# Two gradient stores moved to a scatter by row numbers: a decode-step backward pass on one core

## The chip, the cores and the metric

The kernel runs on one core of one Trainium2 chip. The metric is device time in microseconds (us) of one execution. A core has a matrix engine (TensorE, PE in the profile), three elementwise engines (VectorE = DVE, ScalarE = ACT, GpSimd = POOL), a queue engine that here only issues transfers (SyncE = SP), and 16 DMA engines that move data between the chip's large memory and the on-chip memory of 128 partitions.

## The reference, cut to what matters

The program computes the output and the gradients of a gated mix of two branches for one token: `out = g * attention + (1 - g) * mlp`, with `g = sigmoid(sum(x * gate_w))`, all tensors in bfloat16.

```python
q = (x @ wq).reshape(B, 1, H, Dh)                    # x: 640, H = 32 heads, Dh = 128
p = softmax(q . k_cache * Dh ** -0.5)                # 4096 cached positions per head
a = (p . v_cache).reshape(B, 1, H * Dh) @ wo
act = h * tanh(log1p(exp(-|h|)) + max(h, 0));  h = x @ w1 + b1       # F = 1728
b = act @ w2
```

Returned are the output and the gradients of x, k_cache, v_cache, wq, wo, w1, b1, w2 and gate_w. The gradients of the caches are the bulk: 32 heads of 1 MiB each for K (output 2) and for V (output 3), as much as is read. dw2, the gradient of w2, is output 8, 1728 rows of 640: row i is the i-th activation times one row of 640 numbers that is the same for all.

## The kernel before, in words

One loop goes over the heads. For each head SyncE loads K and V (each 128 partitions x 8,192 B: partition p holds 32 positions), TensorE transposes them, forms score rows (line 538), ScalarE takes exponentials (line 575), VectorE makes the probabilities and their gradients (lines 587 to 593), TensorE multiplies them with K and V (line 631), and VectorE writes the outer products dK and dV (`outer`, line 598), each in two halves. `out_half` calls `outer` and, after the second half, issues the store on SyncE (line 616). There are four buffers for loaded K, four for loaded V, and four for results (`o_sb`). The last heads' results take freed K and V buffers instead, since nothing is loaded into them any more: dV of heads 29 to 31, dK of heads 28 to 30.

The order of the work is written out by hand; a scheduler adds the semaphore waits, and each engine runs its instructions in the written order. The MLP's steps are dealt out over the heads by a small list with costs (`mlp_some`); when its backward part is done, `dw2_some` computes dw2, two of its 14 column groups per head, on ScalarE (`m_dw2`, line 503). It writes dw2 over w2 in the tile `w2_sb`: partition p holds rows 13p to 13p + 12 in the groups 0 to 12 (16,640 B, one piece in the output too), and the last 64 rows stand in group 13. In the loop's pass for head 28 (`h == H - 4`) SyncE stores the first 1,664 rows in three transfers of 4, 4 and 5 groups (line 799), after that head's dV; GpSimd stores the last 64 rows (line 800) and db1 (line 802). GpSimd's own queue reaches line 800 as soon as group 13 is computed, far earlier.

In the same pass the gradients of wo and wq of the group of four heads before are made: four copies on ScalarE (`f_dwo`, line 380) just after that point, products on VectorE (lines 362 and 372). After the loop come head 31, the last group's wq and wo, and the final sums, whose three rows GpSimd stores (lines 920 to 922, 5 rows of 256 B each).

Constants (identity matrices, masks) are made by GpSimd and VectorE in the first 6 us, while the first loads run.

Of the kernel before, what the change touches and what calls it, by code (L numbers as in the profile page):

```python
# [8 lines left out]
ALU = mybir.AluOpType  # L9
AX = mybir.AxisListType  # L10
# [6 lines left out]
def kernel(  # L17
# [24 lines left out]
    nc = tc.nc  # L42
    P = 128
    _, H, Sk, Dh = A_k_cache.shape
# [8 lines left out]
    FR = F // P  # L53
    FM = FR * P
# [4 lines left out]
    W2P = [(0, 4), (4, 8), (8, FR)]  # L59
# [17 lines left out]
    dw2_v = out_8[0:FM, :].rearrange("(p fc) n -> p fc n", p=P)  # L77
# [11 lines left out]
    const = ctx.enter_context(tc.tile_pool(name="const", bufs=1))  # L89
# [59 lines left out]
    w2_sb = const.tile([P, FCN, D], BF16, name="w2_sb")  # L149
    for a, b in W2P:  # L150
# [7 lines left out]
    ident_bf = const.tile([P, P], BF16, name="ident_bf")  # L158
    nc.gpsimd.memset(ident_bf[:], 0.0)
    nc.gpsimd.affine_select(  # L160
        out=ident_bf[:], in_=ident_bf[:], compare_op=ALU.not_equal, fill=1.0,
        base=0, pattern=[[-1, P]], channel_multiplier=1,
# [20 lines left out]
    nc.vector.memset(aT_acc[:], 0.0)  # L183
    bT = const.tile([P, RC], F32, name="bT")
    dx_parts = const.tile([P, RC, NG + 3], F32, name="dx_parts")

    p4b, ds4b = [], []
    qz = const.tile([P, G, 2, 2, 16], BF16, name="qz")
# [57 lines left out]
    def g_qpair_cp(g):  # L246
        pair_cp(qz, groups[g].pop("pair"), 4)

    def g_docol(g):
        groups[g]["col"] = col_mm(groups[g]["do_row"])  # L250
# [163 lines left out]
    def m_np(fc):  # L414
        return P if fc < FR else FT
# [60 lines left out]
    def m_diag():  # L476
        nc.vector.tensor_copy(dh_bf[:, 0:FR], dh32[:, 0:FR])
        nc.vector.tensor_copy(dh_bf[0:FT, FR:FCN], dh32[0:FT, FR:FCN])
        nc.gpsimd.tensor_tensor(diag3, ident_bf[:].unsqueeze(2).to_broadcast([P, P, FR]),
                                dh_bf[:, 0:FR].unsqueeze(1).to_broadcast([P, P, FR]), ALU.mult)  # L480
        nc.gpsimd.tensor_tensor(mjunk[0:FT, FM:F], ident_bf[0:FT, 0:FT],
                                dh_bf[0:FT, FR:FCN].to_broadcast([FT, FT]), ALU.mult)
# [18 lines left out]
    def m_dw2(fc):  # L501
        n = m_np(fc)
        nc.scalar.activation(w2_sb[0:n, fc, :], db_bc[0:n, :], ACT.Copy, scale=act_f[0:n, fc:fc + 1])
# [14 lines left out]
    def ev():  # L518
        trq.pop(0)()
# [6 lines left out]
    def k_pe(h, c):  # L526
        if h < H:
            tr_pe(h, kts, KT, c)

    def v_pe(h, c):  # L530
        if h < H:
            tr_pe(h, vts, VT, c)
# [32 lines left out]
    def softmax(h):  # L565
        mx = s_ps.tile([P, P + 2], F32, name="mx", tag="mx")
        nc.tensor.transpose(mx[:, 0:P], dgms.pop(h)[:].to_broadcast([P, P]), ident_f[:])  # L567
        negM = small.tile([P, 1], F32, name="negM", tag="negM")
        nc.vector.tensor_reduce(negM[:], mx[:, 0:P], axis=AX.X, op=ALU.max, negate=True)  # L569
        return mx, negM  # L570

    def exps(h, negM):
        es[h] = small.tile([P, J], BF16, name="e_bf", tag="e_bf")
        zds[h] = small.tile([P, 2], F32, name="zd", tag="zd")
        nc.scalar.activation(es[h][:], sd[h][0], ACT.Exp, bias=negM[:], scale=scale, accum_out=zds[h][:, 0:1])  # L575
# [21 lines left out]
    def outer(dst, col4, row, a, b):  # L597
        nc.vector.tensor_tensor(  # L598
            dst[:, a:b, :].rearrange("p j (k t) -> p j k t", t=4),
            row.rearrange("p (k t) -> p k t", t=4).unsqueeze(1).to_broadcast([P, b - a, Dh // 4, 4]),  # L600
            col4[:, a:b, :].unsqueeze(2).to_broadcast([P, b - a, Dh // 4, 4]), ALU.mult)

    o_t = {}

    def out_half(w, h, dst, col4, row, k):
        hh = h % G
        if k == 0:
            if w == "k" and H - KBUFS <= h < H - 1:
                o_t[w, h] = kv_in.tile([P, J, Dh], BF16, name="Kn", tag="Kn")
            elif w == "v" and h > H - VBUFS:  # L610
                o_t[w, h] = kv_in.tile([P, J, Dh], BF16, name="Vn", tag="Vn", bufs=VBUFS)
            else:
                o_t[w, h] = outs.tile([P, J, Dh], BF16, name="o_sb", tag="o_sb")
        outer(o_t[w, h], col4, row[:, hh * Dh:(hh + 1) * Dh], k * JH, (k + 1) * JH)
        if k == 1:
            nc.sync.dma_start(dst[h], o_t.pop((w, h))[:])

    def dv_out(h, k):
        out_half("v", h, dVv, p4s[h], groups[h // G]["do_row"], k)
# [1 line left out]
    def dk_out(h, k):  # L621
        if h >= 0:
            out_half("k", h, dKv, ds4s[h], groups[h // G]["qs_row"], k)
# [12 lines left out]
    def dqo_red(h, x):  # L636
        if h >= 0:
            v = x[:].rearrange("p t r -> p (t r)")[:, 3:3 + 4 * (P - 1)].rearrange("p (s q) -> p s q", q=P - 1)
            nc.vector.tensor_reduce(groups[h // G]["dqo"][:, :, h % G],  # L639
                                    v[:, :, 0:P - 1:32].rearrange("p s (i c) -> p i s c", i=2),  # L640
                                    axis=AX.XY, op=ALU.add)
# [6 lines left out]
    m_cost = dict(h=0.8, b1=0.8, act=0.9, b=0.5, dh=0.9, diag=0.5, bc=0.5, dx=0.9, dw1=0.5, gap=0.0)  # L648
    m_fn = dict(h=m_h, b1=lambda i: (m_b1(), m_abs()), act=m_act, b=m_b, dh=m_dh,
                diag=lambda i: m_diag(), bc=m_bc, dx=m_dx, dw1=m_dw1)  # L650
    dw2_next = [0]

    def mlp_some(budget, pause=True):
        spent = 0.0
# [88 lines left out]
    for h in range(H - 1):  # L743
        g, hh = h // G, h % G
        nx, pv = g + 1 < NG, g > 0
        k_pe(h + 1, 2)
        ev()
        mx, negM = softmax(h)
        if hh == 3 and nx:
            g_qpair_cp(g + 1)  # L750
            g_docol(g + 1)
        dqo_red(h - 1, xs[h])
        k_pe(h + 1, 3)
        ev()
        exps(h, negM)
        dk_out(h - 1, 1)
        v_pe(h + 1, 0)
        if hh == 2 and nx:
            g_q(g + 1)
        v_pe(h + 1, 1)  # L760
        if hh == 3 and nx:
            g_dopair(g + 1)
            g_dopair_cp(g + 1)
        k_rows(h + 1)
        ev()
        ev()
        pjs(h)
        v_pe(h + 1, 2)
        ev()
        zd_mm(h, mx)  # L770
        if hh == 0 and pv:
            f_new(g - 1)
            f_diag(g - 1)
        elif h >= 2:
            mlp_some(0.9, False)
        v_pe(h + 1, 3)
        ev()
        probs(h, mx)
        if hh == 0 and pv:
            f_o4(g - 1)  # L780
            f_o4c(g - 1)
            f_bc(g - 1)
        dv_out(h, 0)
        k_pe(h + 2, 0)
        dq_o(h)
        v_rows(h + 1)
        rw_cp(h + 1)
        if h + 2 < H:
            ev()
        dv_out(h, 1)  # L790
        load_k(h + KBUFS)
        load_v(h + VBUFS)
        k_pe(h + 2, 1)
        if h + 2 < H:
            ev()
        if h == H - 4:
            assert dw2_next[0] == FCN
            for a, b in W2P:
                nc.sync.dma_start(dw2_v[:, a:b, :], w2_sb[:, a:b, :])
            nc.gpsimd.dma_start(out_8[FM:F, :], w2_sb[0:FT, FR, :])  # L800
            assert not any(k == "bc" for k, _ in mq)
            nc.gpsimd.dma_start(db1_row, dh_bc[0:1, :])
        if h == H - 2:
            assert not mq
            nc.sync.dma_start(dw1_v[:, 0:3, :], w1_sb[:, 0:3, :])
            nc.sync.dma_start(dw1_v[:, 3:RC, :], w1_sb[:, 3:RC, :])
        dk_out(h, 0)
        x_tr(h + 1)
        maxes(h + 1)
        if hh == 0:  # L810
            if nx:
                g_new(g + 1)
            if pv:
                l_pe(g - 1, 0, G)
                l_add(g - 1, g - 1, True)
                for t in range(G):
                    f_dwo(g - 1, t)
                f_dwo_st(g - 1)
                for c in range(2):
                    f_dx(g - 1, c)  # L820
                    f_dwq(g - 1, c)
        if hh == 1:
            if pv:
                for c in range(2, RC):
                    f_dx(g - 1, c)
                    f_dwq(g - 1, c)
                f_dwq_st(g - 1)
            if nx:
                w_pe("o", g + 1, 0)
                ev()  # L830
                w_pe("o", g + 1, 1)
                ev()
        if hh == 2:
            if g + 2 < NG:
                load_wo(g + 2)
            if not nx:
                for k in range(NWT):
                    w_pe("q", g, k)
                    ev()
            else:  # L840
                w_pe("o", g + 1, 2)
                ev()
                g_do(g + 1)
                g_qcol(g + 1)
                g_qpair(g + 1)
        if hh == 3:
            if g % 2 == 0 and g + 4 <= NG:
                load_wqp(g // 2 + 1)
            if nx:
                g_qs(g + 1)  # L850
        if h >= 2:
            mlp_some(0.9 if hh < 2 else 1.8)
            dw2_some(2)

    g, h = NG - 1, H - 1
# [97 lines left out]
```

## Time and profile before

| | us |
|---|---|
| median of 3 runs (404.71 to 405.26) | 404.71 |
| the profiled execution | 404.96 |
| its span, first to last instruction | 403.2 |
| DMA, busy share of q1 (SyncE's queue) over 16 engines | 98.1% |
| TensorE, VectorE, ScalarE busy | 305.9, 287.9, 232.4 |
| GpSimd busy | 11.8 |
| read and written in large memory | 82.03 MB each, 407 GB/s over the span |

The profile is one execution. Its page shows each engine's busy time, the span in 40 slices with a digit for the busy tenths, the DMA queues, the chain of work that ended last, and the costliest groups of instructions; lines such as L616 are lines of the kernel. Other views of the same trace give a timeline of one engine (start, length, engine, line, operation, out<-in, count, and in brackets the idle time before and what ended it), and tables of windows, one row for each stretch: its length, then busy time and count of PE, PEld (weight loads), DVE, ACT and POOL, TensorE's granted clock, the mean busy share of the 16 DMA engines, and GB/s. The trace also records each semaphore increment; a transfer signals its landing with 16 of them, one for each DMA engine, and the packets of each DMA queue with start, length and size.

### The profile page before, as it was taken

What the parts mean: (1) busy time and instruction counts of PE and PEld (TensorE: products, weight loads), DVE (VectorE), ACT (ScalarE), POOL (GpSimd) and SP (SyncE); (2) the same over time, 40 slices, a digit from 0 to 9 for tenths busy, and PEclk for the clock granted to TensorE, in tenths of its full rate; (3) what the DMA queues carried; (4) which work ended last, traced back from release to release, by engine and by line L of the source; (5) the groups of instructions that cost most, each with busy time, mean ns of one, the idle gap of its engine ahead of it and who ended that gap; (6) DMA issues with size and microseconds to landing.
All of it is one profiled execution on the core that took longest, in us unless ns stands there. A gap on an engine that the chain in (4) does not pass through costs nothing.

```text
span 403.2 us, 7688 instructions
## 1 busy us (share of the span) xinstructions
PE 305.9 (76%) x2930; PEld 207.0 (51%) x2945; DVE 287.9 (71%) x808; ACT 232.4 (58%) x468; POOL 11.8 (3%) x29
## 2 busy tenths in 40 slices
PE   2979989787897985876887779876886977677640
PEld 1556646464565663544555447544555645464420
DVE  2217738868678875769897956896997985679780
ACT  2466757754676563753668667765767655375220
POOL 3000001000000000000001200000000000000001
PEclk9999999988999998989998997988999899889555
DMA  7999999999999999999999999999999999999894
GB/s 274 428 416 423 417 424 415 417 423 424 422 422 426 423 414 424 424 418 428 422 423 428 424 418 424 427 418 423 422 419 424 425 417 425 426 422 377 360 389 153
DMA packets 28708, 164.55 MB, mean 408 GB/s; under 512 B 2991, under 2 KB 3056, under 8 KB 12288
## 3 DMA queue, kind: packets, MB, share of 16 engines
q1 hardware_dynamic: 28256, 163.97, 98.1%
q8 instruction: 23, 0.38, 0.4%
q0 software_dynamic: 384, 0.10, 0.1%
q14 instruction: 13, 0.11, 0.1%
q10 hardware_dynamic: 32, 0.01, 0.0%
HBM read 82.03 MB, written 82.03 MB: 407 GB/s over the span
## 4 chain that ended last, share of the span: by engine, by line
DMA 42%; PE 25%; DVE 22%; ACT 6%; issue 2%; POOL 0%; POOLq 0%; SPq 0%; DVEq 0%; ACTq 0%
DMA out_dram<-o_sb 40%; PE tr L515 9%; DVE o_sb L598 9%; PE rw L538 3%; PE rw L631 3%; DVE junk L362 3%; DMA wq_p<-in_A_wq_dram 2%; PE x L555 2%; DVE wq_p L372 2%; ACT rw_sb L549 2%; ACT do_row L266 2%; PE tr L324 2%; PE do_ps L263 1%; PE h_ps L405 1%; DVE mjunk L494 1%
## 5 line engine op out<-in xcount | busy, mean ns | idle before, releaser
L524 ACT COPY T<-tr 128x512 f32<-128x512 f32 x256 | 138.0, 595 | 53.0 <-PE tr L515 38.3
L598 DVE TENSOR_TENSOR o_sb<-qs_row,ds 128x2048 bf16<-128x2048 bf16 x58 | 70.8, 1220 | 37.6 <-DMA out_dram<-o_sb 37.5
L515 PE MATMUL tr<-ident_f,Kn 128*128 128x128 f32 x512 | 85.6, 295 | 5.8 <-DVE rw L508 5.8
L515 PE MATMUL tr<-ident_f,Vn 128*128 128x128 f32 x512 | 84.5, 299 | 6.6 <-ACT T L524 6.0
L515 PEld LDWEIGHTS tr<-ident_f,Vn 128*128 128x128 f32 x512 | 63.4, 154 | 27.3 <-PE tr L515 12.1
L515 PEld LDWEIGHTS tr<-ident_f,Kn 128*128 128x128 f32 x512 | 61.1, 149 | 23.2 <-PE rw L631 14.1
L598 DVE TENSOR_TENSOR o_sb<-do_row,p 128x2048 bf16<-128x2048 bf16 x58 | 68.2, 1218 | 0.0
L549 ACT COPY rw_sb<-rw 128x512 f32<-128x512 f32 x33 | 19.4, 587 | 51.2 <-PE rw L538 49.0
L631 PE MATMUL rw<-Kn,ds 128*4 128x512 bf16 x256 | 35.9, 405 | 6.4 <-DVE ds L593 5.7
L631 PE MATMUL rw<-Vn,p 128*4 128x512 bf16 x256 | 35.9, 405 | 0.0
L567 PE MATMUL mx<-ident_f,m_s 128*128 128x128 f32 x32 | 10.1, 316 | 29.7 <-DVE m_s L563 29.6
L555 PE MATMUL x<-ident_f,rw_sb 128*128 128x128 f32 x132 | 22.5, 295 | 4.4 <-ACT rw_sb L549 1.4
L362 DVE SCALAR_TENSOR_TENSOR junk<-wq_p,dq_bc 128x512 bf16<-128x512 bf16 x35 | 23.9, 684 | 0.0
L538 PE MATMUL rw<-T,qz 128*32 128x512 bf16 x256 | 22.3, 426 | 0.0
L575 ACT ACTIVATE e_bf<-x,negM 128x32 bf16<-128x32 f32 x32 | 9.3, 292 | 22.4 <-DVE dqo L639 22.1
L567 PEld LDWEIGHTS mx<-ident_f,m_s 128*128 128x128 f32 x32 | 4.5, 142 | 34.0 <-DVE m_s L563 33.9
L538 PE MATMUL rw<-T,doz 128*32 128x512 bf16 x256 | 21.4, 411 | 0.8 <-ACT T L524 0.8
L380 ACT ACTIVATE wo_g<-da_bc,o 128x640 bf16<-128x640 bf16 x28 | 20.9, 816 | 1.2 <-PE ax_ps L350 1.2
L583 PE MATMUL mx<-zd,ones_f 128*128 128x2 f32 x64 | 11.2, 245 | 13.5 <-DVE pj L579 13.4
L555 PEld LDWEIGHTS x<-ident_f,rw_sb 128*128 128x128 f32 x132 | 14.5, 145 | 13.2 <-ACT rw_sb L549 13.2
L569 DVE TENSOR_REDUCE negM<-mx 128x1 f32<-128x128 f32 x32 | 9.2, 288 | 16.1 <-PE mx L567 16.1
L631 PEld LDWEIGHTS <-ds 128*4 128x4 bf16 x256 | 9.1, 85 | 22.2 <-DVE ds L593 11.4
(174 smaller groups left out, 367.6 us busy)
## 6 DMA issues: line engine op xcount, KB each, us to landing
out_dram<-o_sb SPq DMA_DIRECT2D x58, 1024.0 KB, 16.6
Kn<-in_A_k_cache_dram SPq DMA_DIRECT2D x32, 1024.0 KB, 16.8
Vn<-in_A_v_cache_dram SPq DMA_DIRECT2D x32, 1024.0 KB, 17.3
wq_p<-in_A_wq_dram SPq DMA_DIRECT2D x4, 1280.0 KB, 8.7
wo_g<-in_A_wo_dram SPq DMA_DIRECT2D x8, 640.0 KB, 17.6
out_dram<-wo_g SPq DMA_DIRECT2D x8, 640.0 KB, 18.3
out_dram<-wq_p SPq DMA_DIRECT2D x4, 1280.0 KB, 16.3
out_dram<-Kn SPq DMA_DIRECT2D x3, 1024.0 KB, 11.4
```

Of the source, the lines that this page charges most:

```text
L362: nc.vector.scalar_tensor_tensor(jq[:], in0=wqs[g][:, c, :], scalar=1.0, in1=groups[g]["dq_bc"][:], op0=ALU.mult, op1=ALU.mult, accum_out= ...
L380: nc.scalar.activation(wos[g][:, hh, :], da_bc[:], ACT.Copy, scale=groups[g]["o4"][:, hh:hh + 1])
L515: nc.tensor.transpose(tp[:, t, :], words[:, t * P:(t + 1) * P], ident_f[:])
L524: nc.scalar.copy(T[h][:, (3 - c) * (TB // 2):(4 - c) * (TB // 2), :], tp[:])
L538: nc.tensor.matmul(rw[32 * c:32 * (c + 1), :], lhsT=z[:, par, :, :].rearrange("p m u -> p (m u)"), rhs=Tb[:, c, par, :, :], start=first an ...
L549: nc.scalar.copy(rw_sb[h][:].rearrange("p t r -> p (t r)"), rw[:])
L555: nc.tensor.transpose(xs[h][:, 3 - j, :], t[:, j, :], ident_f[:])
L567: nc.tensor.transpose(mx[:, 0:P], dgms.pop(h)[:].to_broadcast([P, P]), ident_f[:])
L575: nc.scalar.activation(es[h][:], sd[h][0], ACT.Exp, bias=negM[:], scale=scale, accum_out=zds[h][:, 0:1])
L583: nc.tensor.matmul(mx[:, P:P + 2], lhsT=ones_f[:], rhs=zds[h][:], start=True, stop=True)
L598: nc.vector.tensor_tensor(dst[:, a:b, :].rearrange("p j (k t) -> p j k t", t=4), row.rearrange("p (k t) -> p k t", t=4).unsqueeze(1).to_br ...
L631: nc.tensor.matmul(rw[32 * c:32 * c + 4, :], lhsT=c4[:, 4 * jb:4 * jb + 16].rearrange("p (j t) -> p t j", t=4)[:, 0, :], rhs=N[:, jb:jb + ...
```

## The change

Two stores leave SyncE's queue. The first 1,664 rows of dw2 and dV of head 29 are now stored by GpSimd: one scatter each, in which partition p goes to the row of the output that an integer in partition p names. For partitions 16 to 19 and 48 to 51 that integer lies past the bound given to the scatter, so they are skipped; each of these two groups of four rows goes by a plain transfer of GpSimd. Row numbers are made once at the start: an iota on GpSimd gives p and 29 * 128 + p, and seven VectorE instructions add 4,096 for the eight partitions. The tile `dx_parts`, not yet in use, serves as scratch.

The column group 0 of dw2 is no longer computed with the others (`dw2_next` starts at 1) but in the pass for head 28, right before the scatter is issued, which therefore waits for it.

```diff
+    LATE = ((16, 20), (48, 52))
+    VSC = H - 3
+    rowids = const.tile([P, 2], mybir.dt.int32, name="rowids")
+    scr = dx_parts[:].rearrange("p c k -> p (c k)")
+    nc.gpsimd.iota(rowids[:], pattern=[[VSC * P, 2]], base=0, channel_multiplier=1)
+    nc.vector.tensor_copy(scr[:, 0:2], rowids[:])
+    for i, (a, b) in enumerate(LATE):
+        nc.vector.reduce_sum(scr[:, 2 + i:3 + i], ident_bf[:, a:b], axis=AX.X)
+    nc.vector.tensor_tensor(scr[:, 2:3], scr[:, 2:3], scr[:, 3:4], ALU.add)
+    nc.vector.tensor_scalar(scr[:, 2:3], scr[:, 2:3], float(H * P), None, ALU.mult)
+    nc.vector.tensor_scalar(scr[:, 0:2], scr[:, 0:2], scr[:, 2:3], None, ALU.add)
+    nc.vector.tensor_copy(rowids[:], scr[:, 0:2])
+
+    def scat_st(i, rows, lim, dst, src):
+        ids = rowids[:, i:i + 1].bitcast(mybir.dt.uint32)
+        nc.gpsimd.indirect_dma_start(out=rows, out_offset=bass.IndirectOffsetOnAxis(ap=ids, axis=0), in_=src,
+                                     in_offset=None, bounds_check=lim - 1, oob_is_err=False)
+        for a, b in LATE:
+            nc.gpsimd.dma_start(dst[a:b], src[a:b])
...
         if k == 1:
-            nc.sync.dma_start(dst[h], o_t.pop((w, h))[:])
+            t = o_t.pop((w, h))
+            if (w, h) == ("v", VSC):
+                rows = out_3.rearrange("b h (p j) d -> (b h p) (j d)", p=P)[0:(h + 1) * P, :]
+                scat_st(1, rows, (h + 1) * P, dst[h].rearrange("p j d -> p (j d)"),
+                        t[:].rearrange("p j d -> p (j d)"))
+            else:
+                nc.sync.dma_start(dst[h], t[:])
...
-    dw2_next = [0]
+    dw2_next = [1]
...
         if h == H - 4:
             assert dw2_next[0] == FCN
-            for a, b in W2P:
-                nc.sync.dma_start(dw2_v[:, a:b, :], w2_sb[:, a:b, :])
+            m_dw2(0)
             nc.gpsimd.dma_start(out_8[FM:F, :], w2_sb[0:FT, FR, :])
+            rows = out_8[0:FM, :].rearrange("(p fc) n -> p (fc n)", p=P)
+            scat_st(0, rows, P, rows, w2_sb[:, 0:FR, :].rearrange("p fc n -> p (fc n)"))
             assert not any(k == "bc" for k, _ in mq)
             nc.gpsimd.dma_start(db1_row, dh_bc[0:1, :])
```

## The prediction

> **What bounds the kernel now.** I read the page's slices and chain first, then the windows of the last 30 us, then the chain and the engines' timelines around the stores that move, then the trace's semaphore increments.
>
> ```profile
> DMA  7999999999999999999999999999999999999894
> DMA 42%; PE 25%; DVE 22%; ACT 6%; issue 2%; POOL 0%; POOLq 0%; SPq 0%; DVEq 0%; ACTq 0%
> ```
>
> The 16 DMA engines are full in all but the first and last slices, and most of the chain is VectorE waiting for the buffer of an earlier store. Up to the last wait of this kind (it ends at 344.4 us) the bytes set the pace. The end is another matter:
>
> ```profile
> 370.00:372.00 2.00, 0.88 (x6) 0.64 (x6) 1.45 (x7) 1.65 (x5) 0.00 (x0) 1.00 0.64 267
> 374.00:376.00 2.00, 1.32 (x9) 0.92 (x6) 1.75 (x2) 0.59 (x1) 0.00 (x0) 0.50 0.46 188
> 376.00:378.00 2.00, 2.00 (x21) 2.00 (x20) 0.55 (x4) 0.71 (x2) 0.00 (x0) 0.50 0.99 385
> 396.00:397.00 1.00, 0.00 (x0) 0.00 (x0) 0.00 (x0) 0.00 (x0) 0.00 (x0) 0.50 0.66 234
> 397.00:398.00 1.00, 0.00 (x0) 0.00 (x0) 0.00 (x0) 0.00 (x0) 0.00 (x0) 0.50 0.09 33
> 398.00:399.00 1.00, 0.00 (x0) 0.00 (x0) 0.00 (x0) 0.00 (x0) 0.00 (x0) 0.50 0.07 25
> 400.00:401.00 1.00, 0.00 (x0) 0.00 (x0) 0.00 (x0) 0.00 (x0) 0.00 (x0) 0.50 0.07 30
> ```
>
> The last two columns are the DMA share and GB/s. From 397 to 402 the share is about 1/16, 25 to 30 GB/s: one DMA engine works alone for some 4.5 us. Before that, the others ran dry (0.64, 0.46) and were full again from 376. The increments agree: a store lands in 16 of them, one for each engine; of the last store (wo_g, line 386) fifteen come by 397.8 us, the sixteenth at 402.2, and the span ends 1.0 later. One engine is last in every transfer from about 200 us on; its distance from the fifteenth grows from 2 us at 237 to 5 us at 354.
>
> Which engine it is, the trace does not say outright. But each of the three last small stores (5 rows of 256 B) has a packet between 398.0 and 399.1, when only the late engine works; the other twelve packets are over by 396.8. So the late engine is one of five that each carry one row of such a 5-row transfer, the same five each time.
>
> **The change, part by part.**
>
> *Relief of the late engine.* Eight of 128 rows are one engine's share of a store. By the sixteenth increments, the three dw2 stores take the late engine from 367.2 to 372.4 (5.2 us) and dV of head 29 from 376.6 to 379.2 (2.6 us): 7.8 us, against a lateness of 4.4. If the rows left out are its share, it stops being last. [...]
>
> *The rows by plain transfers.* Two of 4 x 16,640 B and two of 4 x 8,192 B. By the 5-row stores, each takes one row to each of four engines, the same ones each time: 2 x (16.6 + 8.2) KB at 26.7 GB/s (8 x 8,192 B in 2.45 us) is 1.9 us on each. If the late one is not among them, dw2's 1.25 falls into the idle share before 376 and dV's 0.6 there too or into the full stretch: 0 to 0.6. I take 0.3, the middle. [...]
>
> *GpSimd's issues.* Gone from SyncE's queue: three issues of 0.50 to 1.21 us and one of 0.33. What follows waits for data anyway (the wo_g store leaves at 358.23, when ScalarE ends), so nothing is won.
>
> ```profile
> 354.51 2.87 SPq L799 DMA_DIRECT2D out_dram<-w_sb  x3
> 358.23 0.42 SPq L386 DMA_DIRECT2D out_dram<-wo_g  x1
> 364.73 0.33 SPq L616 DMA_DIRECT2D out_dram<-Vn  x1
> 374.65 0.33 SPq L616 DMA_DIRECT2D out_dram<-Vn  x1
> 375.03 0.43 SPq L805 DMA_DIRECT2D out_dram<-w_sb  x1
> ```
>
> GpSimd's queue gets six: two scatters and four plain issues at 0.50 to 0.57 us. A scatter by row numbers stands nowhere in the trace: below, a plain issue (0.57); above, GpSimd's longest instruction (2.99, line 479). [...] From issue to first packet GpSimd's store of line 800 took 3.7 us.
>
> *The queue behind the scatter.* The scatters name row ranges (all of dw2's first rows; dV of heads 0 to 29) that overlap other stores. If overlapping writes are kept in order, the 4-row transfers wait for their scatter to land, and db1's row and the dV scatter stand behind them on GpSimd. Then: dw2 scatter issued at 356, first packet near 360, 5 us of work per engine shared with wo_g and Kn (4.1): landed near 369; 4-row transfers to 370.5; dV scatter issued near 371.5 instead of 364.7, its packets from 375. Its 2.45 us on each engine then leave the idle share before 376 and enter the full stretch, which has only 0.6 us of idle (shares 0.99, 0.99, 0.98, 0.81, 0.86 of its windows). Cost: 2.45 - 0.6 = 1.85. If they are not ordered: 0. The last stores of GpSimd are at 393.7, long after.
>
> *One ScalarE instruction moved.* m_dw2(0), 0.82 us (line 503), leaves the stretch about 215 us, where DMA hides it, and comes just before the four wo_g copies:
>
> ```profile
> 353.96 1.08 ACT L524 COPY T<-tr 128x512 f32<-128x512 f32 x2
> 355.21 2.99 ACT L380 ACTIVATE wo_g<-da_bc,o 128x640 bf16<-128x640 bf16 x4 [0.17 <-PE ax_ps L350]
> 358.11 1.04 ACT L524 COPY T<-tr 128x512 f32<-128x512 f32 x2
> ```
>
> ScalarE has 0.17 us of idle there and is on the chain, so TensorE's next transposes, and all that follows to the last stores, come 0.65 later. Where the DMA engines are behind by the 1.85 above, this hides under it; without that it is paid. So the two cost between 0.65 and 1.85 together (0 if the chain has slack that it does not show); I take 1.4, nearer the upper end since the ranges do overlap.
>
> [...] While GpSimd ran its 2.99 us multiply, VectorE's line 591 took 2.43 us instead of 0.28:
>
> ```profile
> 221.05 0.22 DVE L589 TENSOR_SCALAR negD<-mx,rz 128x1 f32<-128x1 f32 x1
> 221.19 2.43 DVE L591 TENSOR_SCALAR p<-e_bf,rz 128x128 bf16<-128x128 bf16 x1
> ```
>
> Beside the two issues at 291.9 to 293.0 nothing of VectorE grew. So a scatter's issue costs between 0 and 2.1 us of VectorE; I take 0.2 for the two (the nearer row is the issue).
>
> *Setup.* An iota (0.1 to 0.3 us by the memsets and the select beside it; at worst 2.99) and seven VectorE operations of 0.15 to 0.29 us, 1.0 to 2.0 together, ahead of line 508's memset that ends at 5.65. Covers: TensorE idles 2.08 us until wq_p lands at 9.9, and the loads queued at the start keep the DMA engines full until 42 us while the first store leaves at 34.0. Nothing; without these covers it would be up to 5 us.
>
> *Sum, on the profiled execution* (404.96 us, span 403.2). The second latest engine ends at 397.8, the last 5-row store on it at 398.4. Add 1.4 (queue and ScalarE), 0.3 (rows) and 0.2 (port): 400.3; add 1.0 to the span's end: 401.3 where 403.2 was, a gain of 1.9. With the 1.76 around the span that is 403.05; the median of the three runs (404.71) lies 0.25 under this execution, so **402.8** (a span here stands for a median 1.5 higher). With every unknown at 0 the span is 399.4: 400.9. With 1.85, 0.6 and 2.1 it is 403.95: 405.4, and without the port's 2.1, 403.4.
>
> **Rivals.**
> - *The scatter does not deal its rows as a plain store does* (or the late engine holds other partitions). It then keeps its 7.8 us, its backlog is without a gap from 359 to the end, and neither ScalarE's delay nor the queue touches it: 404.7, within 0.2%. For it: no row shows how a scatter is dealt. Against: eight rows in two groups of four are just one share.
> - *The 4-row transfers go to the late engine.* If it is one of the first four of the five, it keeps its share and gets four more rows, 1.9 us: 406.6. [...]
> - *The scatter moves in small packets: slower.* GpSimd's packets of 5,120 B took 196 ns, those of 216 B 16 ns, half the rate. 3.1 MB at half the rate cost 7.3 us more on every engine, less the 2.1 idle before 376 (shares 0.84, 0.64 and 0.46 of three windows of 2 us from 368): the others end near 403.0, the small stores and the rows 0.9 later, the span at 404.9, so 406.4. It decides where the rate falls under 0.57 of SyncE's (5.6 us more of work). For it: many row numbers at one byte offset each. Against: a row is 8 or 16 KB in one piece.
>
> **How the numbers follow.** Measurement tells about 0.2% (0.8 us). Relief works: 0.60, of which 0.04 ends within 0.2% because the port or the queue eats it. Not relieved: 0.17, of which 0.12 within 0.2% and 0.05 slower. Four rows on the late engine: 0.08, slower. Small packets or a long scatter: 0.15, slower. So faster 0.56, same 0.16, slower 0.28. The likeliest case has its own range, 400.9 to 404.0; to leave out no more than 2 in 10, it goes from 400.8 to 406.2.
>
> **What would show it.** Right: no stretch at 1/16 share at the end, fifteenth and sixteenth increments within 1 us of each other after 375, some 3.1 MB more on the software queue, line 503 once at 355 us with wo_g behind it, the dV scatter near 371 if the queue holds. Wrong: the stretch stays (first rival) or grows (second), the software queue's packets are small or the share sags between 360 and 375 (third), or VectorE's operations stretch beside GpSimd's issues.

## The result and the profile after

The changed kernel is slower: 409.48 us median (408.4 to 410.95, 5 runs) beside 404.71 us (404.65 to 405.26, 5 runs) for the kernel before, a ratio of 1.0118 (1.0106 to 1.013). The forecast was 402.8 us, with a range up to 406.2. The profiled execution took 409.48 us, its span 407.1.

First the page: the queues of the kernel after (packets, MB, share of 16 engines' span).

```profile
span 407.1 us, 7721 instructions
q1 hardware_dynamic: 27680, 160.79, 95.3%
q0 software_dynamic: 800, 3.28, 2.4%
```

GpSimd's queue (q0) now carries 3.28 MB, as the change says. Its 2.4% will matter below: another kernel moves the same 800 packets and 3.28 MB in 2.0%.

Then GpSimd's timeline around the moved stores.

```profile
356.02 1.06 POOL L202 DMA_INDIRECT out_dram<-w_sb,rowids  x1 [64.61 <-ACT w_sb L523]
367.96 1.11 POOL L205 DMA_DIRECT2D out_dram<-w_sb  x2 [10.88 <-DMA out_dram<-w_sb,rowids]
369.06 0.52 POOL L829 DMA_DIRECT2D out_dram<-dh_bc  x1
369.99 1.05 POOL L202 DMA_INDIRECT out_dram<-Vn,rowids  x1 [0.41 <-DMA out_dram<-Kn]
381.05 1.07 POOL L205 DMA_DIRECT2D out_dram<-Vn  x2 [10.01 <-DMA out_dram<-Vn,rowids]
```

L202 is a scatter, L205 its two 4-row transfers. A scatter takes 1.05 us of GpSimd. The brackets show that the 4-row transfers do wait for their scatter to land, and that dV's scatter leaves behind them, at 369.99. This part went as forecast (371.5 where the queue holds).

The windows tell where the time is (the last two columns are the DMA share and GB/s; before them stand the stretch's length, five pairs of busy time and count, and TensorE's clock).

```profile
368.00:370.00 2.00, 1.71 (x18) 0.85 (x15) 1.93 (x8) 0.30 (x1) 1.59 (x4) 1.00 0.64 194
370.00:372.00 2.00, 0.57 (x5) 0.57 (x6) 1.52 (x6) 1.83 (x5) 1.04 (x1) 1.00 0.35 104
397.00:398.00 1.00, 0.00 (x0) 0.00 (x0) 0.00 (x0) 0.00 (x0) 0.00 (x0) 0.50 0.69 261
398.00:399.00 1.00, 0.00 (x0) 0.00 (x0) 0.00 (x0) 0.00 (x0) 0.00 (x0) 0.50 0.33 133
400.00:401.00 1.00, 0.00 (x0) 0.00 (x0) 0.00 (x0) 0.00 (x0) 0.00 (x0) 0.50 0.26 100
402.00:403.00 1.00, 0.00 (x0) 0.00 (x0) 0.00 (x0) 0.00 (x0) 0.00 (x0) 0.50 0.25 100
404.00:405.00 1.00, 0.00 (x0) 0.00 (x0) 0.00 (x0) 0.00 (x0) 0.00 (x0) 0.50 0.09 36
405.00:406.00 1.00, 0.00 (x0) 0.00 (x0) 0.00 (x0) 0.00 (x0) 0.00 (x0) 0.50 0.03 10
```

Before, the end was a stretch at 1/16 share: one engine alone. Now it is a stretch at 4/16, 100 GB/s: four engines alone from about 400.4 to 403.1, then three, two, one. The semaphore increments of the last large store (wo_g, 16 each, us) say the same:

```
before  fourteen by 397.1, then 397.8, 402.2
after   ten by 398.0, then 398.9, 400.4, 403.1, 404.0, 404.8, 405.8
```

Where one engine was late, four now are. The packets of the 4-row transfers show what happened to them. Each scatter packet took 620 ns (16,640 B) or 309 ns (8,192 B, both medians of 120), 26.8 and 26.5 GB/s. The plain packets of the same sizes took (in the order of their starts):

```
16,640 B, us   2.35 2.44 2.32 1.28 2.78 3.88 3.63 3.91   sum 22.57, a quarter 5.6 (forecast 1.25)
 8,192 B, us   1.88 0.46 0.96 2.05 2.34 2.35 1.95 1.52   sum 13.49, a quarter 3.4 (forecast 0.61)
```

No more than four of them ran at once. Spread over four engines, four packets on each, that is 9.0 us on each instead of the 1.9 forecast. What remained was why.

### The profile page after: what moved, and what is told of

Its sections match the earlier page's. It is cut to its first block, busy times and chain, and to the rows that moved or that the text cites. A ratio compares the mean times of both kernels' runs of the same rounds, so it can differ in the third digit from the quotient of the medians.

```text
span 407.1 us, 7721 instructions
## 1 busy us (share of the span) xinstructions
PE 307.7 (76%) x2945; PEld 208.2 (51%) x2945; DVE 288.9 (71%) x815; ACT 232.9 (57%) x468; POOL 16.2 (4%) x36
## 3 DMA queue, kind: packets, MB, share of 16 engines
q0 software_dynamic: 800, 3.28, 2.4%
HBM read 82.03 MB, written 82.22 MB: 403 GB/s over the span
## 4 chain that ended last, share of the span: by engine, by line
DMA 45%; DVE 24%; PE 21%; ACT 5%; issue 2%; POOL 0%; POOLq 0%; SPq 0%; DVEq 0%; ACTq 0%
DMA out_dram<-o_sb 39%; DVE o_sb L618 8%; PE tr L535 7%; DMA Kn<-in_A_k_cache_dram 3%; DVE junk L382 3%; PE rw L657 3%; PE rw L558 3%; DMA wq_p<-in_A_wq_dram 2%; DVE wq_p L392 2%; PE x L575 2%; ACT do_row L286 2%; PE tr L344 1%; PE do_ps L283 1%; ACT rw_sb L569 1%; PE h_ps L425 1%
## 5 line engine op out<-in xcount | busy, mean ns | idle before, releaser
L535 PE MATMUL tr<-ident_f,Vn 128*128 128x128 f32 x512 | 86.6, 305 | 6.3 <-ACT T L544 5.8
L535 PE MATMUL tr<-ident_f,Kn 128*128 128x128 f32 x512 | 84.6, 292 | 5.7 <-DMA Kn<-in_A_k_cache_dram 5.7
L535 PEld LDWEIGHTS tr<-ident_f,Vn 128*128 128x128 f32 x512 | 65.3, 157 | 27.2 <-PE tr L535 13.0
```

The lines of the kernel that those rows point to most:

```text
L535: nc.tensor.transpose(tp[:, t, :], words[:, t * P:(t + 1) * P], ident_f[:])
```

## The experiments

Two explanations fit so far. **P**: partitions 16 to 19 (and 48 to 51) share one way out of the on-chip memory, which carries about what one DMA engine can take; four engines that read there at once get a quarter each. **D**: plain transfers of four rows from GpSimd's queue are slow wherever they read. A third cause, **Q**, could add to either: the queue wait that moved dV's scatter. The runs of the first four kernels share 20 runs of the kernel before (median 404.88), the other four share 15 (404.74).

**The same rows, read through other partitions.** The kernel after, with one line changed.

```diff
-            nc.gpsimd.dma_start(dst[a:b], src[a:b])
+            nc.gpsimd.dma_start(dst[a:b], src[a:a + 16:4])
```

> The changed kernel, but each plain transfer reads partitions 16, 20, 24, 28 (and 48, 52, 56, 60) instead of 16 to 19 (and 48 to 51); rows, destinations, queue and waits stay, so the eight rows hold other rows' data. Theory P (four neighbouring partitions share one way out of the on-chip memory that carries about one DMA engine's rate, so four engines that read them at once get a quarter each, and what is queued behind them on these engines waits): the 16,640 B packets take 0.62 to 0.8 us instead of 1.3 to 3.9, the four late engines are late no more, 402 to 403.5 us. Theory D (a plain transfer of 4 rows from GpSimd is slow wherever it reads: neighbouring destination rows, or the software queue): packets of 2 to 4 us stay, 409 us. Theory Q (the dV scatter that waits behind the dw2 scatter on GpSimd is what costs): packets fast, but 407 us or more.

Measured: 403.64 us, ratio 0.9963 (0.9949 to 0.9977): faster than before, 5.8 us under the kernel after. The profiled execution was the slowest of its five (404.99 us, span 403.0). Its queue line and its end:

```profile
q0 software_dynamic: 800, 3.28, 2.0%
398.00:399.00 1.00, 0.00 (x0) 0.00 (x0) 0.00 (x0) 0.00 (x0) 0.00 (x0) 0.50 0.71 275
399.00:400.00 1.00, 0.00 (x0) 0.00 (x0) 0.00 (x0) 0.00 (x0) 0.00 (x0) 0.50 0.15 54
400.00:401.00 1.00, 0.00 (x0) 0.00 (x0) 0.00 (x0) 0.00 (x0) 0.00 (x0) 0.50 0.03 10
```

The plain 16,640 B packets now took 0.62 to 0.64 us each, the 8,192 B ones 0.49 to 0.75. The 4/16 stretch is gone. Queue, sizes, count and destination are those of the kernel after; only the partitions read differ. D falls, and P stands.

**The rows left out.**

```diff
-        for a, b in LATE:
-            nc.gpsimd.dma_start(dst[a:b], src[a:b])
```

> The changed kernel without the four plain transfers: the 16 rows of partitions 16 to 19 and 48 to 51 are not stored at all, and the dV scatter no longer waits for the dw2 scatter to land. Theories P and D: the late engine is relieved and nothing takes its place, 401 to 402.5 us, 0.5 to 1.5 under the run with other partitions. Theory Q: 401 to 402.5 here too, since its wait is gone, but 4 us or more under the run with other partitions.

Measured: 402.53 us, 0.9936 (0.992 to 0.9953); span 400.7, wo_g's last two increments at 398.1 and 399.1. Without the 4-row transfers dV's scatter leaves at 368.51 us, against 370.86 in the experiment above. Between these two kernels lie 1.1 us, which hold the rows at their full speed and these 2.4 us of the later dV scatter together, so this part of Q is small. The scatter still leaves 3.8 us later than dV's store in the kernel before (364.73): its range of rows covers dV of heads 0 to 29, and the trace shows GpSimd's queue waiting until dV of head 28 has landed (sixteenth increment at 367.62, wait over at 367.64). What this rest costs was not tried by itself.

```profile
396.00:397.00 1.00, 0.00 (x0) 0.00 (x0) 0.00 (x0) 0.00 (x0) 0.00 (x0) 0.50 1.01 409
397.00:398.00 1.00, 0.00 (x0) 0.00 (x0) 0.00 (x0) 0.00 (x0) 0.00 (x0) 0.50 0.32 107
398.00:399.00 1.00, 0.00 (x0) 0.00 (x0) 0.00 (x0) 0.00 (x0) 0.00 (x0) 0.50 0.03 10
```

**Nothing skipped.** All 128 rows by the scatter, no plain transfers; this is the scatter without its purpose.

```diff
-    nc.vector.tensor_scalar(scr[:, 0:2], scr[:, 0:2], scr[:, 2:3], None, ALU.add)
...
-        for a, b in LATE:
-            nc.gpsimd.dma_start(dst[a:b], src[a:b])
```

> The changed kernel with all 128 rows in both scatters and no plain transfers, so no engine is relieved. Theories P and D: the scatter itself costs nothing, the one late engine of the kernel before is back and sets the end, 404.5 to 405.5 us, with one engine alone for some 4 us at the end. If the scatter (its descriptors, GpSimd's port) is what costs: 407 us or more.

Measured: 405.68 us, 1.0018 (1.0008 to 1.0027). One late engine is back, with wo_g's last increments at 399.5, 400.3 and 402.4:

```profile
399.00:400.00 1.00, 0.00 (x0) 0.00 (x0) 0.00 (x0) 0.00 (x0) 0.00 (x0) 0.50 0.12 47
400.00:401.00 1.00, 0.00 (x0) 0.00 (x0) 0.00 (x0) 0.00 (x0) 0.00 (x0) 0.50 0.07 29
401.00:402.00 1.00, 0.00 (x0) 0.00 (x0) 0.00 (x0) 0.00 (x0) 0.00 (x0) 0.50 0.05 20
```

So it is the skipping of partitions 16 to 19 and 48 to 51 that relieves the late engine (last increment at 399.1 with it, 402.4 without), and these are its share. In this kernel dV's scatter left only at 373.49, 4.9 us after dw2's last scatter packet had ended. The same wait for dV of head 28 held it: the late engine's increment of that store, the sixteenth, came at 372.60, and the wait in GpSimd's queue was over at 372.62. So the late engine delayed the scatter too.

**Only the ScalarE instruction moved.** The kernel before, with column group 0 of dw2 computed in the pass for head 28, ahead of SyncE's three stores.

```diff
-    dw2_next = [0]
+    dw2_next = [1]
...
             assert dw2_next[0] == FCN
+            m_dw2(0)
             for a, b in W2P:
```

> The kernel before with one part of the change alone: group 0 of dw2 is computed in the pass for head 28, ahead of SyncE's three stores. All theories: the late engine's backlog covers it, 404.5 to 405.2 us, while the wo_g copies on ScalarE and the last products come 0.4 to 0.7 us later. If ScalarE's delay is the cost: 406 us or more.

Measured: 404.98 us, 1.0001 (0.9992 to 1.0011). ScalarE's timeline of this kernel:

```profile
354.27 1.08 ACT L524 COPY T<-tr 128x512 f32<-128x512 f32 x2
355.22 0.85 ACT L503 ACTIVATE w_sb<-db_bc,act_f 128x640 bf16<-128x640 bf16 x1
355.96 2.98 ACT L380 ACTIVATE wo_g<-da_bc,o 128x640 bf16<-128x640 bf16 x4
```

The wo_g copies start 0.75 us later than before (355.21), and fourteen engines end 0.7 later (397.8 instead of 397.1), while the late engine ends where it did (402.3 and 402.2). But 0.31 of this stood already before the moved instruction (the copies of line 524 start at 354.27, before at 353.96), so about 0.44 belongs to the move, which was priced at 0.65. The late engine hides it.

**Four rows that lie 32 apart.** Partitions 16, 48, 80 and 112 are read.

```diff
-            nc.gpsimd.dma_start(dst[a:b], src[a:b])
+            nc.gpsimd.dma_start(dst[a:b], src[16:128:32])
```

> The changed kernel, but both plain transfers of each scatter read partitions 16, 48, 80 and 112, one every 32 (the eight rows hold other rows' data). [...] If only neighbouring partitions get in each other's way, they take 0.62, as with partitions 16, 20, 24 and 28, and the time is that run's 403.6.

Measured: six 16,640 B packets took 1.47 to 1.76 us, the two on the engine that began 1.2 us after the others 0.62 and 0.76. All eight ran between 369.37 and 371.96: 133,120 B in 2.6 us, 51 GB/s, the rate of two engines (2 x 26.8). So at a distance of 32 the four rows did not come out at the full rate of four engines, as they did at a distance of four (0.62 to 0.64 us), but at half of it. Which of the four partitions hinder each other is not shown; that it is a partition and the one 32 above it is the author's estimate. The time was 403.33 us, 0.996 (0.9944 to 0.9975), 0.3 under the first experiment in spite of the slower packets: the 4.7 us on each of the four engines (11.33 and 7.63 us in all, over four) are not told apart from the 2.5 of the first experiment. The windows from 368 to 372, in which the engines run dry (shares 0.56 and 0.38), have room for the 2.8 us of dw2's rows.

**Four other neighbours.** Partitions 64 to 67 and 96 to 99, where the late engine has no share.

```diff
+            c = 64 if a == 16 else 96
-            nc.gpsimd.dma_start(dst[a:b], src[a:b])
+            nc.gpsimd.dma_start(dst[a:b], src[c:c + 4])
```

> The changed kernel, but the plain transfers read partitions 64 to 67 and 96 to 99 instead of 16 to 19 and 48 to 51 (the eight rows hold other rows' data). Theory P for any group of four: packets of 1.3 to 3.9 us again, four engines late, 408 to 410.5 us. If the slowness belongs to the group that starts at 16 (its own engine is the late one of the kernel before): packets near 0.62 us, 403.6.

Measured: 409.08 us, 1.0094 (1.0078 to 1.0109), as slow as the kernel after. Packets of 2.18 to 4.74 us (16,640 B), 10.6 us on each of four engines, and the same end:

```profile
q0 software_dynamic: 800, 3.28, 2.5%
399.00:400.00 1.00, 0.00 (x0) 0.00 (x0) 0.00 (x0) 0.00 (x0) 0.00 (x0) 0.50 0.33 134
401.00:402.00 1.00, 0.00 (x0) 0.00 (x0) 0.00 (x0) 0.00 (x0) 0.00 (x0) 0.50 0.31 122
403.00:404.00 1.00, 0.00 (x0) 0.00 (x0) 0.00 (x0) 0.00 (x0) 0.00 (x0) 0.50 0.27 108
```

So the late engine's partitions are not slow by themselves: another set of four neighbours, read by four engines, is as slow. This trace also shows the sharing from the other side. While the four rows of partitions 96 to 99 were read (371.64 to 376.81), eight packets of dV's scatter, one behind the other from 371.93 on and so on one engine, took 0.53 to 0.64 us instead of 0.31. Eight packets are one engine's share of 128; that they are the rows of partitions 64 to 67 and 96 to 99, which this scatter does not skip, is the author's estimate, since the trace does not name a packet's partition. Five engines are late in this kernel, not four: wo_g's last increments are at 402.5, 404.8, 405.4, 405.5 and 406.4, the other eleven by 399.3.

**dw2 alone.** dV of head 29 goes back to SyncE's queue whole.

```diff
-            if (w, h) == ("v", VSC):
-                rows = out_3.rearrange("b h (p j) d -> (b h p) (j d)", p=P)[0:(h + 1) * P, :]
-                scat_st(1, rows, (h + 1) * P, dst[h].rearrange("p j d -> p (j d)"),
-                        t[:].rearrange("p j d -> p (j d)"))
-            else:
-                nc.sync.dma_start(dst[h], t[:])
+            nc.sync.dma_start(dst[h], t[:])
```

> The changed kernel with dV of head 29 back on SyncE's queue, so only dw2 goes by scatter and plain rows. Theory P: the four engines that carry the rows lose about 22.6 us over four, 5.6 each, part of it in the idle share before 376, and dV's 3.4 each in the full stretch is saved: 404.5 to 406.5 us. If dw2's rows alone are enough for the whole loss: 408 or more.

Measured: 405.28 us, 1.0008 (0.9999 to 1.0017): no difference that can be measured. The eight packets took 2.25 to 4.52 us (sum 29.1, so 7.3 on each of four engines).

```profile
374.00:376.00 2.00, 1.32 (x17) 0.24 (x6) 2.00 (x3) 0.58 (x1) 0.00 (x0) 0.50 0.73 172
376.00:378.00 2.00, 2.00 (x15) 1.94 (x16) 1.10 (x5) 0.06 (x1) 0.00 (x0) 0.50 0.16 57
399.00:400.00 1.00, 0.00 (x0) 0.00 (x0) 0.00 (x0) 0.00 (x0) 0.00 (x0) 0.50 0.31 124
400.00:401.00 1.00, 0.00 (x0) 0.00 (x0) 0.00 (x0) 0.00 (x0) 0.00 (x0) 0.50 0.20 79
```

Part of this falls into the dry stretch, the rest is the 0.31 and 0.20 at the end, where wo_g's last five increments lie between 400.1 and 401.9. What the relief of dw2's share wins, the same rows by plain transfers take back.

**dw2's late rows from elsewhere.** If P is right, the rows must leave through many partitions. One ScalarE instruction, in the pass for head 26, computes the eight rows of 13 x 640 numbers once more as 104 pieces of 640, one on each of the partitions 0 to 103 of a tile that is free then; eight small transfers of GpSimd bring the factors there beforehand. The two plain transfers store 52 pieces each. dV of head 29 stays with SyncE, and of column group 0 only 16 columns are computed late.

```diff
-        for a, b in LATE:
-            nc.gpsimd.dma_start(dst[a:b], src[a:b])
+        for i, (a, b) in enumerate(LATE):
+            nc.gpsimd.dma_start(out_8[FR * a:FR * b, :], late_sb[NL * i:NL * i + NL, :])
...
+    NL, TAIL = 4 * FR, 16
+    late_act, late_sb = mt[0][:, 0:1], mjunk[:, 0:D]
+    def m_late_act():
+        for i, (a, b) in enumerate(LATE):
+            for j in range(4):
+                p = NL * i + FR * j
+                nc.gpsimd.dma_start(late_act[p:p + FR, :], act_f[a + j:a + j + 1, 0:FR])
+    def m_late_rows():
+        nc.scalar.activation(late_sb[0:2 * NL, :], db_bc[0:2 * NL, :], ACT.Copy, scale=late_act[0:2 * NL, :])
...
+        if h == H - 6:
+            m_late_rows()
         if h == H - 4:
-            m_dw2(0)
+            m_dw2_tail()
```

> A version that uses the cause: only dw2 goes by scatter, without the eight rows; these are computed a second time, as 104 pieces of 640 numbers on partitions 0 to 103 (one ScalarE instruction of 0.82 us in the pass for head 26, the factors brought there by eight transfers of 13 numbers), and stored by two plain transfers of 52 pieces each. So they leave the on-chip memory by many ways and by thirteen engines, 10 KB each. Only the last 16 columns' worth of group 0 (its first 16 columns) is computed late. Theory P: the late engine is 5.2 us lighter, its lateness was 4.4, nobody takes its place: 400.8 to 402.3 us, faster than before. If relief of one engine buys nothing: 404.5 to 405.

Measured: 402.48 us, 0.9938 (0.9924 to 0.9951), faster than both kernels. GpSimd's timeline, then the windows at the end:

```profile
356.31 1.57 POOL L202 DMA_INDIRECT out_dram<-w_sb,rowids  x1 [63.46 <-ACT w_sb L541]
369.41 1.14 POOL L205 DMA_DIRECT2D out_dram<-mjunk  x2 [11.53 <-DMA out_dram<-w_sb,rowids]
```

```profile
396.00:397.00 1.00, 0.00 (x0) 0.00 (x0) 0.00 (x0) 0.00 (x0) 0.00 (x0) 0.50 0.85 324
397.00:398.00 1.00, 0.00 (x0) 0.00 (x0) 0.00 (x0) 0.00 (x0) 0.00 (x0) 0.50 0.13 53
398.00:399.00 1.00, 0.00 (x0) 0.00 (x0) 0.00 (x0) 0.00 (x0) 0.00 (x0) 0.50 0.02 5
```

wo_g's fourteenth to sixteenth increments are at 397.6, 398.4 and 398.8; the stretch with one engine alone has shrunk from 4.4 us to 0.4. By the packet counts of the pages (of 2 to 8 KB 9,232 before, 384 of them SyncE's stores of dw2, and 8,874 now) the two plain transfers moved in 26 packets, so 13 of 5,120 B each; that each of the 13 lay on an engine of its own is the author's estimate. This kernel does in the sum what the change wanted, with dw2's relief alone (5.2 us against a lateness of 4.4).

Four runs came out above the range expected of them, each by less than 0.2 us: 403.64 (at most 403.5 expected), 402.53 (402.5), 405.68 (405.5) and 402.48 (402.3).

## Why the prediction was wrong, by its steps

- *Relief of the late engine*: right. The store of Kn in which it landed last at 376.6 now landed by 371.5, and the kernel without the plain rows, which skips, takes 402.53 us where the one without the skip takes 405.68 (part of these 3.2 us is the later dV scatter of the second, which waited for the late engine).
- *The rows by plain transfers*: **this step failed.** It let each 4-row transfer run at 26.7 GB/s on each of four engines, a rate taken from stores that read all 128 partitions, and priced the 1.9 us per engine at 0.3. The rate did not hold where four engines read four neighbouring partitions: the packets took 9.0 us per engine. Four engines went into the last stores late, and were still 5.1 to 7.8 us behind the rest at the end. No rival of the prediction had this mechanism: each spoke of the late engine or of the scatter. The experiments order the 16,640 B packets by the partitions that are read at once: 0.62 to 0.64 us at 16, 20, 24, 28 and at 48, 52, 56, 60, mostly 1.47 to 1.76 at 16, 48, 80, 112, and 1.3 to 4.7 at four neighbours, whether 16 to 19 and 48 to 51 or 64 to 67 and 96 to 99. The prediction asked whether the eight partitions are the late engine's share, and not what happens to four engines that read four of them at once.
- The same four engines were taken by all four plain transfers, as the prediction read from the 5-row stores: four are held by them, not eight or sixteen (the share at the end is 0.25 to 0.26). Whether the late engine is one of the four is not shown; the increments at 398.9 and 400.4 outside the four speak for "no". The one at 400.4 may be the late engine itself, whose own share is these partitions: from 372.43 on six packets of SyncE's queue (8,192 B), one behind the other, took 0.61 to 0.63 us instead of 0.31 while the plain rows were read, but the trace does not name their engine.
- *GpSimd's issues*: 1.06 and 1.05 us for a scatter; both lie within the forecast's bounds of 0.57 and 2.99. In the other kernels it was up to 1.57, and 2.02 once in the first experiment.
- *The queue behind the scatter, and the ScalarE instruction*: the order was as described (dV's scatter at 369.99, forecast 371.5), and the size too large: together with the 0.2 for the port 1.6 us, where ten engines end their wo_g at 397.8 to 398.0 instead of 396.9 to 397.1, about 0.9. The wait for dV of head 28 (landed at 367.3) was over before the 4-row transfers left, so it cost nothing here.
- *GpSimd beside VectorE, and the setup*: no run shows the port to which the sum gives 0.2 us. Beside the scatters (356.02 to 357.08 and 369.99 to 371.04) nothing of VectorE grew: line 382 took 0.68 us, line 392 0.35 and line 618 1.22, as in the kernel before (lines 362, 372 and 598). The iota took 0.13 us. Both were small, as priced.
- *The sum.* 398.4 with 0.9 in place of 1.6 gives 399.3; the last increment came at 405.8, so the rows cost 6.5 where 0.3 stood; the span ended 1.3 later at 407.1, 5.8 above the forecast's 401.3. The median lies 2.4 above the span, where 1.5 was taken: this is the other 0.9 of the 6.7 us.
- Where the step is put right by reading the rows through partitions 16, 20, 24, 28 and 48, 52, 56, 60, the kernel takes 403.64 us, 0.8 from the forecast. That it comes so near is in part luck, since the queue and ScalarE were priced too high.
- *Rivals*: that the scatter is not dealt as a plain store is out (it took 620 ns a row, and its skipping relieved the late engine), and so is that it moves in small packets. The end that came resembles the second rival, rows on an engine that ends last, but on four engines and at about a quarter of the rate (packets of 2.8 us on the mean instead of 0.62); that the late engine keeps its share, as this rival has it, the runs with and without the skip speak against (402.53 and 405.68 us).

## To carry to other kernels

The rate of a DMA engine in a profile was measured with a pattern of partitions, and here it changed with the pattern. Before a few rows are split off into a small transfer, ask which partitions its engines will read at the same time: four neighbours gave each engine about a quarter of its rate here (a 16,640 B packet took 2.8 us on the mean), and four partitions that lie four apart the full one (0.62 to 0.64 us). Relief for one late engine is only worth as much as what does the work in its place, so look for the next late one, too.

## What the runs showed that was not expected

- The eight rows of 16,640 B from partitions 16 to 19 and 48 to 51 would take 8 x 0.62 = 5.0 us at the rate of one DMA engine. In the kernel after they took from 369.14 to 376.41, 7.3 us, and the six slowed packets of SyncE's queue (0.61 to 0.63 us instead of 0.31) ran in the same time. Together these are 182,272 B, 25 GB/s, about the 26.8 of one engine. So a few rows read in this way held up not only the four engines that read them but also, by these packets, another engine; that its store was reading the same partitions is the author's estimate. No such row of slowed packets of SyncE's queue stands in the kernels that read the rows through other partitions.
- The large memory's written bytes are 82.22 MB in the page of the kernel after, 82.03 before, though the stores cover the same rows. The difference is 198,656 B, exactly the 16 plain rows (8 x 16,640 B and 8 x 8,192 B); with dw2's eight alone it is 133,120 B, their 8 x 16,640 B. With the rows left out the page says 82.03 again, though these rows are not stored at all. So the page counts a scatter with the rows that it skips, and the plain transfers come on top.
- A scatter by 128 row numbers costs GpSimd mostly about as much as two plain issues (1.03 to 1.57 us, once 2.02, beside 1.07 to 1.21), and the rows beyond its bound left their engine free: with them skipped wo_g's last increment came at 399.1, with them stored by the scatter at 402.4.
